# A gated dilated-attention kernel: the transfers of weights, values, queries and keys spread out, and all of feature group 2 by seven products

## The chip, the cores and the metric

The kernel runs on one NeuronCore of one Trainium2 chip. Its time is the device time of an execution in microseconds; before the change three runs gave 748.61, 748.99 and 751.39 us, median 748.99. One further execution was taken with the hardware profiler. The engines are named as the profile names them: PE (TensorE, matrix products), PEld (its weight loads), DVE (VectorE), ACT (ScalarE), POOL (GpSimd) and SP (SyncE, which mostly issues transfers).

## What is computed

x has 2048 positions of 640 features. The reference, cut to what matters:

```python
xn = layernorm(x)
# 32 heads of 20 features, a window of 8 positions, 2 apart, looking back
q, k, v = split(xn @ wqkv)
logits = einsum("bhsd,bhswd->bhsw", q, k[window]) * 20 ** -0.5   # masked before position 0
s = einsum("bhsw,bhswd->bhsd", softmax(logits), v[window]).reshape(1, 2048, 640) @ wo
h = (xn @ w_gate) * (xn @ w_up)          # 1536 features
out = x + s * silu(h @ w_down)
```

## The kernel before

All products run on PE with numbers split into a high and a low part (ACT copies the high part, POOL or DVE subtracts it: L109 and L110 for weights, L1008 and L1012 for attention's output), so a product of two split operands is three matmuls per 128 rows.

**Products by seven.** Several stages treat their matrices as two by two blocks and take seven block products instead of eight (Strassen's scheme). The price is sums and differences of the blocks ahead of the products and additions behind them. `differences` forms the input sums T1 to T4 of four chunks of 512 positions, and stores those of chunks 0 and 1 in main memory (t_scr, and e_scr for T4).

**The stages, in the order of PE's work.** Layernorm statistics and the first feature groups; the q, k, v products in rounds (`qkv`, L428); gate and up for twelve groups of 128 features (`group`, or `gate` and `up`); the output projection in pairs of tiles (`pair_product`, L1033); the down projection by seven products (L896); and the final gating. The input is cut into four chunks of 512 positions.

**Feature groups.** Groups 0 and 1 use plain products. For the groups 3 to 10 `group(f, 2)` takes chunks 2 and 3, then `group(f, 0, 1)` takes chunks 0 and 1, each with seven products: 54 matmuls of 512 columns. Group 2 uses seven products for chunks 2 and 3 and plain products (`gate`, `up`: L119) for chunks 0 and 1: 60 matmuls. `two(f)` says which way a group goes, by the number F_TWO. The weights of a group arrive whole (`load_wf`, 640 KB), `w_add` forms their sums (S and R), `w_split` splits G (gate), U (up), S and R. ACT copies a finished product out (`hold`, L1295), DVE adds and multiplies (`gate_a`, `gate_b` L1298, `up_a`), and `up_b` and `h_b` (L1301, L1304) run on POOL for chunks 2 and 3 and for early groups, on DVE otherwise: `eng = nc.vector if c0 and f >= VEC else nc.gpsimd`. A group's result goes to main memory (h_scr).

**Transfers of T.** `load_t(n)` brings one third of T1 to T3 of chunks 0 and 1 (768 KB) from t_scr, `load_e` half of T4 (512 KB) from e_scr. Both are issued by POOL, in its own order of work.

**Attention.** `attention` is a generator that works through twelve units (a group of heads and one of the two dilation phases, in ORDER) on DVE and POOL: the products q times k (L527), their sums (L534), softmax, then the products with the values (L498) and their accumulation on POOL (L504). One round overlaps the scores of one unit with the values of the unit before. It is not a stage of its own: whoever issues PE work calls `advance(credits)`, and the generator emits steps until its credits are spent. The order of instructions on DVE, POOL and ACT is therefore fixed by where these calls stand. `ahead(n, parts)` issues loads of a unit in SP's queue: part 0 is its queries and keys, part 1 its values, both into two alternating kv buffers. `store_o` writes a unit's result to o_scr.

**Early sums.** `early_sums` forms sums for the T inputs on POOL. EARLY of these steps are issued ahead of `scales(8)` (L278 to L334), whose result PE needs for a product of 32 columns (L340).

**The output projection.** `turn_pair(p)` transposes the two tiles of a pair on DVE (L710) and forms four sums (L982 to L985). `hi_pair` and `lo_pair` split the sums. `split_wo(k)` splits sums of the output weights; `sums_wo` forms them. The pair products' results are added by DVE (L1039 to L1044). `wd_sums` (L797 to L809) prepares the weights of the down projection.

**Dictionaries of places.** `places[second, n]` and `beside[f, second, n]` hold functions that are called behind the n-th product of a group's half (second 0: chunks 2 and 3; second 1: chunks 0 and 1).

Of the kernel before, what the change touches and what calls it, by code (L numbers as in the profile page):

```python
# [19 lines left out]
P = 128  # L20
S, D, F = 2048, 640, 1536
# [23 lines left out]
PACE = 1.0  # L45
VEC = 3
EARLY = 3
GROUP_RATE = 0.184
# [8 lines left out]
def kernel(  # L57
# [316 lines left out]
    ORDER = [0, 1, 2, 3, 4, 6, 5, 7, 8, 11, 9, 10]  # L374
    wide, now = [], [None]
    q_t, kv_t, kv_buf, kv_zero, scr, staged, made = {}, {}, {}, {}, {}, [], set()
# [43 lines left out]
    def qkv(m, r, i, runs=ALL_RUNS, at=None, act=None, bank=("q", 3)):  # L420
# [9 lines left out]
        if m or r:  # L430
            if not staged:
                y = slot([P, 2, 2 * 3 * CMAX], F32)
                staged.extend([y[:, 0], y[:, 1], st([P, 2 * 3 * CMAX], "pk", 1)])
            if c > CMAX and not wide:
                wide.extend([slot([P, 6 * c], F32), st([P, 6 * c], "pk", 1)])
            if i % 2 == 0:
                now[0] = wide if c > CMAX else staged
                now[0].insert(0, now[0].pop())
            n = len(MADE[m])
            y = now[0][0][:, :6 * c].rearrange("p (n a i c) -> p n a i c", n=n, a=3, i=2)  # L440
            nc.scalar.activation(y[:, :, :, i % 2, :].rearrange("p n a c -> p a n c"),
                                 p.rearrange("p (a n c) -> p a n c", a=3, n=n), AF.Copy)
# [18 lines left out]
    def attention():  # L461
# [45 lines left out]
        for n, u in enumerate(ORDER + [None]):  # L507
            if u is not None:
                late_unit = u not in made
                while u not in made:  # L510
                    yield None
                ahead(n, (0, 1))
                for _ in range(5 if late_unit else 0):
# [8 lines left out]
            for j in PAIRS:  # L522
                if u is not None:
                    ahead(n + 1, (0,))
                    k = flat(kv[:, 0, j:j + NE, :])
                    k = bass.AP(k.tensor, k.offset, [k.ap[0], [c, 2], k.ap[1]])
                    nc.vector.tensor_mul(t, q, k)  # L527
                    yield 2 * NE * c * 1.22e-3
# [12 lines left out]
            if u is None:  # L541
                store_o(before)
                ring[:] = three
                return
            ahead(n + 1, (0, 1))
            if before is not None:
# [617 lines left out]
    f0, f1 = KF - 2, KF - 1  # L1164
    F_TWO = 3
    tt, tw, steps = {0: [], 2: []}, {}, []
# [120 lines left out]
    def group(f, c0=0, second=0):  # L1287
# [26 lines left out]
        if not second:  # L1314
            if not two(f - 1):
                w_split(f, "U")
            w_sum.pop(f, None)
            wf_raw.pop(f)
            if f < f1 and f + 1 not in wf_raw:
                load_wf(f + 1)  # L1320
        for n, j in enumerate((0, 5, 2, 1, 4, 3, 6)):
# [18 lines left out]
            if (f, second, n) in beside:  # L1340
                beside[f, second, n]()
            advance(PACE * len(runs) * (GROUP_RATE if two(f) else 0.184))

# [35 lines left out]

    def next_sums(f):  # L1380
        w_split(f, "S", "R")
        w_sum.pop(f)
        if f < f1:
            load_wf(f + 1)

    def first_parts():
# [3 lines left out]
        w_split(2, "S")  # L1390
        yield
        w_split(2, "G")
        yield
# [5 lines left out]
    for m, t in ((m, t) for m in range(1, len(MADE)) for t in range(DIL)):  # L1399
# [3 lines left out]
        for i in range(NE):  # L1403
# [7 lines left out]
            if (m, r, i) == (last - 1, 1, 6):  # L1411
                load_wf(2)
            qkv(m, r, i)
            if i == 1:
                finish_piece()
# [7 lines left out]
        elif (m, r) == (last, 1):  # L1423
            for k in range(2):
# [5 lines left out]
    beside.update({(f0, 0, 5): lambda: advance(1e9), (f0, 1, 0): lambda: begin_last(), (f0, 1, 1): lambda: load_pair(0),  # L1430
                   (f0, 1, 4): lambda: sums_wo(), (f0, 1, 5): lambda: split_wo(0, nc.vector),
                   (f0, 1, 6): lambda: split_wo(1, nc.vector)})

# [15 lines left out]
    def load_late(n):  # L1449
        if n < 2:  # L1450
            load_t(n + 2)
        else:
            load_e(1, n - 2, n - 2)

    for f in range(2, f1):
        places.clear()
        if not two(f):
            places.update({(0, 3): sums("S1", "S2"), (0, 4): sums("S3", "d5", "S4")})
            if two(f + 1):
                places.update({(0, 0): lambda f: load_t(0), (0, 2): lambda f: load_t(1)})  # L1460
            group(f, 2)
            next_sums(f + 1)
            g0 = gate(f, 0)
            g1 = gate(f, 1)
            if two(f + 1):
                tw.pop("G")
            w_split(f + 1, "G")
            up(f, 0, g0)
            up(f, 1, g1)
            if two(f + 1):  # L1470
                tw.pop("U")
# [32 lines left out]
    g3 = gate(f1, 3)  # L1504
    turn_pair(2)
    up(f1, 3, g3)
# [25 lines left out]
    for p in range(SP // 2):  # L1532
# [142 lines left out]
```

## Time and profile before

| | |
|---|---|
| median of three runs | 748.99 us (748.61 to 751.39) |
| profiled execution | 748.28 us |
| its span | 746.5 us |
| PE busy | 735.4 us (99%) |
| DVE busy | 612.2 us (82%) |
| POOL busy | 462.6 us (62%) |
| ACT busy | 302.5 us (41%) |
| granted clock of PE | 1.00 in every stretch asked for |

All times in the text are microseconds from the start of the span. A row of the timeline gives start, duration, engine, line, operation, output<-inputs, the shape and how many instructions were merged; a bracket at its end says how long the engine stood before it, and for whom. A row of the grouped view ends with busy time and mean nanoseconds of one, then the idle time before the group. Names of tiles are those of buffers that are used again and again (s, t, xc, kv, wraw, gh, o), so one name has many uses.

Where the stages lie in this execution: the q, k, v products end at 273.9; chunks 2 and 3 of group 2 run from 273.9 to 286.1, its chunks 0 and 1 from 286.1 to 299.7; groups 3 to 10 follow, with attention beside them until about 489; the pair products run from 525.8 on.

### The profile page before, as it was taken

To read this page: it belongs to the slowest core of one execution; us is meant where nothing else is said; L and a number is where in the kernel's file an instruction comes from. 1 tells how busy PE (TensorE), PEld (TensorE's weight loads), DVE (VectorE), ACT (ScalarE), POOL (GpSimd) and SP (SyncE) were. 2 spreads that over 40 slices of the span, in tenths; PEclk is the share of its full clock that TensorE was granted. 3 is DMA by queue.
4 is the path that set the end of the run, shared out by engine and by line. 5 is a ranking of instruction groups with operands and counts; after the bars stand their busy time and mean duration, and the time that the engine had idled before them with its cause. 6 is when DMAs were issued, how large, how long until landed. Compare 5 with 4: busy or idle time off the path is not lost. (4 is left out here: it accounts for less than half of the span.)

```text
span 746.5 us, 11102 instructions
## 1 busy us (share of the span) xinstructions
PE 735.4 (99%) x4054; PEld 669.0 (90%) x4054; DVE 612.2 (82%) x720; ACT 302.5 (41%) x577; POOL 462.6 (62%) x389
## 2 busy tenths in 40 slices
PE   8999999999999999999999999999999999999997
PEld 6989989988999998778887888887899999999997
DVE  7666998699697887998999999667998777777775
ACT  5658413323332332233223322335556564444442
POOL 6169929787688878888879989877559800000000
PEclk9999999999999999999999999999999999999999
DMA  9465672947446548856165424268567655555534
GB/s 316 170 202 200 236 224 87 299 157 239 127 152 197 190 128 232 274 161 207 55 159 149 115 82 110 72 178 204 167 177 212 228 220 191 191 191 191 191 106 141
DMA packets 103493, 132.98 MB, mean 178 GB/s; under 512 B 22696, under 2 KB 74404, under 8 KB 103438
## 3 DMA queue, kind: packets, MB, share of 16 engines
q1 hardware_dynamic: 84686, 112.77, 48.4%
q10 hardware_dynamic: 17600, 14.26, 5.9%
q0 software_dynamic: 1152, 5.24, 2.2%
q8 instruction: 32, 0.52, 0.3%
q14 instruction: 23, 0.19, 0.1%
HBM read 83.58 MB, written 47.81 MB: 176 GB/s over the span
## 5 line engine op out<-in xcount | busy, mean ns | idle before, releaser
L504 POOL TENSOR_TENSOR o<-o,t 128x960 f32<-128x960 f32 (+1 forms) x69 | 139.6, 2024 | 19.1 <-DVE t L498 17.6
L498 DVE TENSOR_TENSOR t<-e,kv 128x960 f32<-128x960 f32 (+1 forms) x96 | 99.4, 1037 | 24.8 <-POOL o L504 24.7
L527 DVE TENSOR_TENSOR t<-q,kv 128x1920 f32<-128x1920 f32 (+1 forms) x48 | 92.4, 1925 | 4.3 <-DMA kv<-qkv_scr 4.2
L534 DVE TENSOR_REDUCE lg<-t 128x96 f32<-128x1920 f32 (+1 forms) x48 | 92.3, 1922 | 0.2
L428 PE MATMUL q<-s,xc 128*128 128x360 f32 (+1 forms) x450 | 83.1, 334 | 0.6 <-DVE lg L266 0.5
L110 POOL TENSOR_TENSOR s<-wraw,s 128x384 fp32r<-128x384 f32 (+6 forms) x58 | 69.6, 1210 | 19.9 <-ACT s L109 19.9
L428 PEld LDWEIGHTS q<-s,xc 128*128 128x128 f32 x450 | 74.9, 188 | 4.8 <-DVE lg L266 0.8
L1295 ACT ACTIVATE gh<-g 128x512 f32<-128x512 f32 x54 | 32.2, 597 | 115.8 <-PE g L1328 97.8
L428 PE MATMUL u<-s,xc 128*128 128x360 f32 (+1 forms) x360 | 65.8, 334 | 0.0
L428 PEld LDWEIGHTS u<-s,xc 128*128 128x128 f32 x360 | 60.3, 188 | 2.3
L428 PE MATMUL g<-s,xc 128*128 128x360 f32 (+1 forms) x330 | 61.5, 337 | 0.0
L428 PEld LDWEIGHTS g<-s,xc 128*128 128x128 f32 x330 | 55.7, 188 | 2.6
L1328 PE MATMUL u<-xc,s 128*128 128x512 f32 x216 | 55.3, 391 | 0.9 <-ACT gh L1295 0.9
L896 PE MATMUL q<-xc,s 128*128 128x320 f32 x342 | 55.5, 309 | 0.0
L1328 PE MATMUL g<-s,s 128*128 128x512 f32 x216 | 55.0, 390 | 0.0
L896 PEld LDWEIGHTS q<-xc,s 128*128 128x128 f32 x342 | 51.5, 188 | 0.0
L1328 PEld LDWEIGHTS u<-xc,s 128*128 128x128 f32 x216 | 40.3, 188 | 10.5 <-ACT gh L1295 2.0
L1328 PEld LDWEIGHTS g<-s,s 128*128 128x128 f32 x216 | 40.5, 188 | 8.6 <-ACT gh L1295 0.2
L109 ACT ACTIVATE s<-wraw 128x384 fp32r<-128x384 f32 (+6 forms) x59 | 33.5, 587 | 29.5 <-PE g L1328 9.0
L504 POOL TENSOR_TENSOR o<-t 128x960 f32<-128x960 f32 (+1 forms) x12 | 24.4, 2032 | 31.8 <-DVE t L498 25.2
L1328 PE MATMUL g<-xc,s 128*128 128x512 f32 x168 | 41.5, 391 | 1.3 <-ACT gh L1295 1.3
L119 PE MATMUL g<-xc,s 128*128 128x512 f32 (+1 forms) x180 | 40.1, 373 | 0.0
(367 smaller groups left out, 1566.5 us busy)
## 6 DMA issues: line engine op xcount, KB each, us to landing
h_scr<-gh SPq DMA_DIRECT2D x48, 256.0 KB, 2.6
wraw<-in_wgu SPq DMA_DIRECT2D x11, 640.0 KB, 4.4
kv<-qkv_scr SPq DMA_DIRECT2D x14, 480.0 KB, 5.9
qkv_scr<-s ACTq DMA_DIRECT2D x18, 360.0 KB, 4.4
t<-h_scr SPq DMA_DIRECT2D x8, 768.0 KB, 7.1
kv<-qkv_scr SPq DMA_DIRECT2D x14, 367.5 KB, 6.6
s_scr<-gh SPq DMA_DIRECT2D x16, 320.0 KB, 4.2
gh<-s_scr SPq DMA_DIRECT2D x16, 320.0 KB, 3.5
```

The lines of the kernel that those rows point to most:

```text
L109: nc.scalar.activation(hi, raw, AF.Copy)
L110: eng.tensor_sub(lo, raw, hi.bitcast(F32))
L119: nc.tensor.matmul(acc, a, b, start=first and n == 0, stop=last and n == len(runs) - 1)
L428: nc.tensor.matmul(p, xT[(r * NE + i) // TPC][a][:, k, t0:t0 + P], wq[m][b][k], start=n == 0, stop=n == len(runs) - 1, skip_group_check=ac ...
L498: nc.vector.tensor_mul(t.rearrange("p (n d) -> p n d", d=DH), e[:, :, w].unsqueeze(2).to_broadcast([P, NE * nh, DH]), v)
L504: return NE * c * cost, lambda: eng.tensor_add(y, z, t)
L527: nc.vector.tensor_mul(t, q, k)
L534: nc.vector.tensor_reduce(out=lg[:, :, j:j + 2].rearrange("p n a -> p a n"), in_=t.rearrange("p a (n d) -> p a n d", d=DH), op=ALU.add, ax ...
L896: nc.tensor.matmul(p, y[:, i, k], wd_t[name][k][:, l], start=new and r == 0, stop=r == len(runs) - 1, skip_group_check=True)
L1295: nc.scalar.activation(kept[j], b["ACACABA"[j]], AF.Copy)
L1328: nc.tensor.matmul(y, w, x, start=j in (0, 1, 5) and r == 0, stop=r == len(runs) - 1, skip_group_check=True)
```

## The change

1. F_TWO goes from 3 to 2: chunks 0 and 1 of group 2 are taken by `group(2, 0, 1)`, 54 matmuls in place of 60. Group 2's G weights use the single "pk" buffer, which served as a third staging buffer of the q, k, v outputs until then; it leaves that use at the seventh tile from the end of the last round, and G is split at the third from the end.
2. The T transfers come earlier: `load_t(0)` in the last q, k, v round, the second and third load behind the first product of `group(2, 2)`, the fourth behind the second, both `load_e` behind the third. Before, two were issued in `group(2, 2)` and the others in `group(3, 2)`.
3. In attention, the values of a unit are asked for at j = 2 of its own round, and the queries and keys of the next from j = 4 on; before, both were asked for as soon as their buffers allowed, the values at the end of the round before, ahead of that round's store.
4. The weights of a group are asked for behind the first product of the group before it, rather than at its start; those of group 2 in the second last q, k, v round, as before, but the queue's neighbours differ.
5. VEC goes from 3 to 2: `up_b` and `h_b` of group 2's chunks 0 and 1 run on DVE.
6. EARLY goes from 3 to 1.
7. `split_wo(0)` goes one place later, to where `split_wo(1)` stands.
8. `turn_pair(2)` goes from between the last `gate` and `up` to behind `lo_pair(1, 0)` in the first turn of the pair loop.

The program has six matmuls of 512 columns fewer and three DVE additions more.

How the instructions move, at three places. The first is POOL's order around group 2. Line 1182 (1186 after) is a T transfer, the next transfer line an E transfer; L504 (L505) is attention's accumulation, L1272 (L1276) a weight sum, L110 the low part of a split (s: U, S or R; pk: G). Before, from the splits of group 2 on:

```order
L110 TENSOR_TENSOR s_2634<-wraw_2294,s_2634 128x384
L110 TENSOR_TENSOR s_2641<-wraw_2232,s_2641 128x640
L1182 DMA s_2652<-t_scr 128x1536
L389 MEMSET kv_124 1x840
L1182 DMA s_2686<-t_scr 128x1536
L1272 TENSOR_TENSOR wraw_2699<-wraw_2637 128x256
```

and later, in group 3:

```order
L110 TENSOR_TENSOR s_2634<-wraw_2637,s_2634 128x384
L1182 DMA s_2854<-t_scr 128x1536
L389 MEMSET kv_124 1x840
L1182 DMA s_2874<-t_scr 128x1536
L1186 DMA xc_449<-e_scr_109 128x1024
L1186 DMA xc_449<-e_scr_110 128x1024
```

After, in group 2 alone:

```order
L1186 DMA s_2536<-t_scr 128x1536
L505 TENSOR_TENSOR o_2427<-o_2427,t_938 128x640 x2
L110 TENSOR_TENSOR pk_2583<-wraw_2223,pk_2583 128x640
L505 TENSOR_TENSOR o_2427<-o_2427,t_938 128x640 x3
L110 TENSOR_TENSOR s_2633<-wraw_2289,s_2633 128x384
L110 TENSOR_TENSOR s_2633<-wraw_2223,s_2633 128x384
L1186 DMA s_2650<-t_scr 128x1536
L1186 DMA s_2652<-t_scr 128x1536
L1186 DMA s_2665<-t_scr 128x1536
L1190 DMA xc_449<-e_scr_109 128x1024
L1190 DMA xc_449<-e_scr_110 128x1024
```

One T transfer now stands in the last q, k, v round; the three others and both E transfers stand in a row behind group 2's splits.

The second is SP's queue where a unit's store (o_scr) meets the loads for the units that follow (kv: keys or values, q: queries). Before:

```order
L175 DMA wraw_3407<-in_wgu 128x1280
L1284 DMA h_scr<-gh_3324 128x4x128
L1284 DMA h_scr<-gh_3349 128x4x128
L414 DMA kv_124<-qkv_scr_2086 128x960
L416 DMA kv_124<-qkv_scr_2086 112x840
L416 DMA kv_124<-qkv_scr_2086 15x840
L575 DMA o_scr<-o_3163 128x8x80
L575 DMA o_scr<-o_3163 128x8x40
L408 DMA q_3468<-qkv_scr_2463 128x960
L414 DMA kv_1029<-qkv_scr_2463 128x960
```

After:

```order
L175 DMA wraw_3414<-in_wgu 128x1280
L579 DMA o_scr<-o_3154 128x8x80
L579 DMA o_scr<-o_3154 128x8x40
L1288 DMA h_scr<-gh_3408 128x4x128
L1288 DMA h_scr<-gh_3439 128x4x128
L414 DMA kv_124<-qkv_scr_2086 128x960
L416 DMA kv_124<-qkv_scr_2086 112x840
L416 DMA kv_124<-qkv_scr_2086 15x840
L1288 DMA h_scr<-gh_3502 128x4x128
```

The store stands ahead of the value loads, and these two result stores (h_scr) behind it; the next unit's queries come after.

The third is DVE's order at the first pair products. L710 (L714) is a transpose, L982 to L985 (L986 to L989) the four sums of a turn, L797 and L800 (L801, L804) weight sums, L1012 (L1016) a low part, L1039 and L1042 (L1043, L1046) additions of a pair's results. Before:

```order
L985 TENSOR_TENSOR s_4483<-s_4483 128x256
L710 STREAM_TRANSPOSE s_4525<-s_4459 128x640 x2
L982 TENSOR_TENSOR s_4459<-s_4525 128x256
L983 TENSOR_TENSOR s_4459<-s_4459,s_4525 128x256
L984 TENSOR_TENSOR s_4459<-s_4525,s_4459 128x256
L985 TENSOR_TENSOR s_4525<-s_4525 128x256
L797 TENSOR_TENSOR lg_4567<-wraw_4494 128x320
L800 TENSOR_TENSOR lg_4568<-wraw_4494,lg_4567 128x320
L1012 TENSOR_TENSOR xc_4552<-s_4483,xc_4552 128x640
L1039 TENSOR_TENSOR gh_4599<-o_4554,u_4571 128x320
L1042 TENSOR_TENSOR gh_4611<-o_4554,q_2_66 128x320
```

After:

```order
L989 TENSOR_TENSOR s_4478<-s_4478 128x256
L801 TENSOR_TENSOR lg_4555<-wraw_4489 128x320
L804 TENSOR_TENSOR lg_4556<-wraw_4489,lg_4555 128x320
L1016 TENSOR_TENSOR xc_4540<-s_4478,xc_4540 128x640
L714 STREAM_TRANSPOSE s_4569<-s_4454 128x640 x2
L986 TENSOR_TENSOR s_4454<-s_4569 128x256
L987 TENSOR_TENSOR s_4454<-s_4454,s_4569 128x256
L988 TENSOR_TENSOR s_4454<-s_4569,s_4454 128x256
L989 TENSOR_TENSOR s_4569<-s_4569 128x256
L1043 TENSOR_TENSOR gh_4594<-o_4542,u_4559 128x320
L1046 TENSOR_TENSOR gh_4606<-o_4542,q_2_66 128x320
```

The turn of pair 2 (s_4525 before, s_4569 after) now stands between the first low part and the first two additions of results.

The diff, cut to its core:

```diff
-VEC = 3
-EARLY = 3
+VEC = 2
+EARLY = 1
...
-                staged.extend([y[:, 0], y[:, 1], st([P, 2 * 3 * CMAX], "pk", 1)])
+                stage_pk.append(st([P, 2 * 3 * CMAX], "pk", 1))
+                staged.extend([y[:, 0], y[:, 1], stage_pk[-1]])
...
-                ahead(n, (0, 1))
+                ahead(n, (0, 1) if late_unit else (0,))
...
             for j in PAIRS:
                 if u is not None:
-                    ahead(n + 1, (0,))
+                    if j == 2:
+                        ahead(n, (1,))
+                    elif j > 2:
+                        ahead(n + 1, (0,))
...
-            ahead(n + 1, (0, 1))
+            ahead(n + 1, (0,))
             if before is not None:
                 store_o(before)
...
-    F_TWO = 3
+    F_TWO = 2
...
             w_sum.pop(f, None)
             wf_raw.pop(f)
-            if f < f1 and f + 1 not in wf_raw:
-                load_wf(f + 1)
...
                 beside[f, second, n]()
+            if (second, n) == (0, 0) and f < f1 and f + 1 not in wf_raw:
+                load_wf(f + 1)
...
             qkv(m, r, i)
+            if m == last and n == NT - 7:
+                staged[:] = [y for y in staged if y is not stage_pk[-1]]
+            elif m == last and n == NT - 5:
+                load_t(0)
+            elif m == last and n == NT - 3:
+                w_split(2, "G")
...
-                   (f0, 1, 4): lambda: sums_wo(), (f0, 1, 5): lambda: split_wo(0, nc.vector),
-                   (f0, 1, 6): lambda: split_wo(1, nc.vector)})
+                   (f0, 1, 4): lambda: sums_wo(), (f0, 1, 6): lambda: (split_wo(0, nc.vector), split_wo(1, nc.vector))})
...
     def load_late(n):
-        if n < 2:
-            load_t(n + 2)
+        if n == 0:
+            load_t(1)
+            load_t(2)
+        elif n == 1:
+            load_t(3)
         else:
-            load_e(1, n - 2, n - 2)
+            load_e(1, 0, 0)
+            load_e(1, 1, 1)
 
     for f in range(2, f1):
         places.clear()
-        if not two(f):
...
-            group(f, 2)
-            next_sums(f + 1)
-            g0 = gate(f, 0)
-            g1 = gate(f, 1)
...
-            up(f, 0, g0)
-            up(f, 1, g1)
...
-            continue
         places.update(two_places)
         if f == F_TWO:
-            places.update({(0, n): lambda f, n=n: load_late(n) for n in range(4)})
+            for n in range(3):
+                places[0, n] = lambda f, n=n: load_late(n)
         group(f, 2)
         group(f, 0, 1)
...
     g3 = gate(f1, 3)
-    turn_pair(2)
     up(f1, 3, g3)
...
             lo_pair(p + 1, 0)
+            if not p:
+                turn_pair(2)
```

More of the change, by code (lines that the diff above doesn't have):

```diff
@@ L374 @@
     ORDER = [0, 1, 2, 3, 4, 6, 5, 7, 8, 11, 9, 10]
-    wide, now = [], [None]
+    wide, now, stage_pk = [], [None], []
     q_t, kv_t, kv_buf, kv_zero, scr, staged, made = {}, {}, {}, {}, {}, [], set()
@@ L1378, in up @@
         advance(PACE * 2.8)
[L1380 to L1384, printed above, removed]
     def first_parts():
@@ L1390, in first_parts @@
         w_split(2, "S")
-        yield
-        w_split(2, "G")
         yield
@@ L1449, in load_late @@
     def load_late(n):
-        if n < 2:
-            load_t(n + 2)
-        else:
-            load_e(1, n - 2, n - 2)
+        if n == 0:
[3 more added lines that the diff above has]
+            load_t(3)
+        else:
+            load_e(1, 0, 0)
+            load_e(1, 1, 1)
     for f in range(2, f1):
         places.clear()
-        if not two(f):
-            places.update({(0, 3): sums("S1", "S2"), (0, 4): sums("S3", "d5", "S4")})
-            if two(f + 1):
-                places.update({(0, 0): lambda f: load_t(0), (0, 2): lambda f: load_t(1)})
-            group(f, 2)
-            next_sums(f + 1)
-            g0 = gate(f, 0)
-            g1 = gate(f, 1)
-            if two(f + 1):
-                tw.pop("G")
-            w_split(f + 1, "G")
-            up(f, 0, g0)
-            up(f, 1, g1)
-            if two(f + 1):
-                tw.pop("U")
-            continue
         places.update(two_places)
         if f == F_TWO:
-            places.update({(0, n): lambda f, n=n: load_late(n) for n in range(4)})
+            for n in range(3):
+                places[0, n] = lambda f, n=n: load_late(n)
         group(f, 2)
```

## The prediction

> **What bounds the kernel.** I read the head of the page first: the span, the busy time of each engine, and the chain that ended last.
>
> ```profile
> span 746.5 us, 11102 instructions
> ...
> PE 735.4 (99%) x4054; PEld 669.0 (90%) x4054; DVE 612.2 (82%) x720; ACT 302.5 (41%) x577; POOL 462.6 (62%) x389
> ...
> PE 28%; DVE 2%; issue 1%; POOL 1%; DMA 0%; ACT 0%; SPq 0%; DVEq 0%; ACTq 0%
> ```
>
> TensorE is busy for 735.4 of 746.5 us. So a change can gain only in two ways: fewer matmuls, or less of the 11.1 us in which TensorE stands. What it does on DVE, POOL and the queues counts only where TensorE then waits. The second view is therefore who TensorE waited for, as a sum and then in time order.
>
> ```profile
> PE q L224 <- POOL lg masks.py:199: 1.4, 1, 1.4
> PE g L1328 <- ACT gh L1295: 1.3, 2, 0.9
> PE e L340 <- POOL lg L334: 1.0, 1, 1.0
> PE u L1328 <- ACT gh L1295: 0.9, 2, 0.6
> ```
>
> ```profile
> 49.46 0.41 PE L340 MATMUL e<-lg,lg 128*128 128x32 f32 x2 [1.03 <-POOL lg L334]
> ...
> 286.14 3.56 PE L119 MATMUL g<-xc,s 128*128 128x512 f32 x15
> 289.54 3.56 PE L119 MATMUL u<-xc,s 128*128 128x512 f32 x15
> ...
> 323.53 2.35 PE L1328 MATMUL g<-xc,s 128*128 128x512 f32 x9 [0.47 <-ACT gh L1295]
> ...
> 334.34 1.89 PE L1328 MATMUL u<-xc,s 128*128 128x512 f32 x7 [0.30 <-ACT gh L1295]
> ...
> 398.90 1.43 PE L1328 MATMUL g<-xc,s 128*128 128x512 f32 x5 [0.87 <-ACT gh L1295]
> ...
> 508.01 2.34 PE L1328 MATMUL u<-xc,s 128*128 128x512 f32 x9 [0.60 <-ACT gh L1295]
> ...
> 533.96 0.56 PE L1033 MATMUL e<-s,xc 128*128 128x320 f32 x2 [0.78 <-DVE xc L1012]
> 534.75 1.15 PE L1033 MATMUL q<-xc,kv 128*128 128x320 f32 x6 [0.23 <-DVE gh L1042]
> ```
>
> The first wait (1.4 us, at the program's start) isn't touched. The brackets of the timeline, 4.3 us in all, lie where this change works. Every term below is one of these brackets or a new one.
>
> **Six matmuls fewer.** Chunks 0 and 1 of group 2 take 54 matmuls of 512 instead of 60. Fifteen of them last from 286.14 to 289.54, 0.227 us each: 6 x 0.227 = 1.36 us, all on TensorE's path. **-1.36.**
>
> **One early sum instead of three.** L334 lets TensorE go at 49.46.
>
> ```profile
> 43.79 2.55 POOL L593 TENSOR_TENSOR kv<-xc 128x512 f32<-128x512 f32 x2 [17.92 <-DVE xc L370]
> ...
> 47.55 0.21 POOL L278 TENSOR_TENSOR lg<-lg 128x4 f32<-128x4 f32 x1
> ...
> 49.17 0.24 POOL L334 TENSOR_TENSOR lg<-mro,lg 128x32 f32<-128x32 f32 x1
> ```
>
> The scale chain (47.55 to 49.41) stands behind three sums on POOL (43.79 to 47.55). Two of them, 2.5 us, go behind it, so it ends near 46.9; TensorE would arrive at 49.46 - 1.03 = 48.43. The wait goes whole. The sums put back are not late next: the same POOL work stands between this chain and the next. **-1.03.**
>
> **The T loads.** They move from group 3 to group 2: T1 to T3 of chunks 0 and 1 are now read in group 2's second half, which starts at 286.14. POOL issues the second, third and fourth load and both E loads in one go, behind the R and U splits.
>
> ```profile
> 261.20 1.56 POOL L110 TENSOR_TENSOR s<-wraw,s 128x640 fp32r<-128x640 f32 x1
> ...
> 277.45 2.55 POOL L110 TENSOR_TENSOR s<-wraw,s 128x384 fp32r<-128x384 f32 x2
> ```
>
> ```profile
> L1182 POOL DMA_DIRECT2D s<-t_scr x4: 527/564/758, 279.9 to 307.9; - x4
> ...
> DMA to landing us min/median/max: 8.8/10.6/11.7
> ```
>
> The 2.55 us are a split of 384 columns and one of 640; the second alone is 1.56, so 384 cost 0.99. Both are 384 wide afterwards and end at 277.45 + 1.98 = 279.4. Issues follow at 0.56 us (the median of the L1182 row): 279.4, 280.0, 280.5. TensorE reads the second load in its third product, at 286.14 + 15 x 0.227 = 289.54, the third two matmuls later, at 290.0, the fourth after 15 more, at 292.9. With the shortest landing all are there: no wait. With the median the third comes at 290.6 (0.6 us), with the longest at 291.7 (1.7 us). The loads go out in a row, so I take a value between the median and the longest. **+1.0, ends 0 and +1.7.**
>
> [...]
>
> **What the old T transition cost.** ACT held its copies back at 323.53 and 334.34, where group 3 reads the T tiles for the first time with its stores behind their loads: 0.77 us together. The same crowd now stands in group 2. I take half as moved. **-0.4, ends -0.77 and +0.4.**
>
> **The order in SP's queue.** The store of an attention round now goes ahead of the next value load.
>
> ```profile
> 392.59 2.26 POOL L504 TENSOR_TENSOR o<-t 128x960 f32<-128x960 f32 x1 [5.39 <-DMA o_scr<-o]
> ```
>
> POOL stood 5.39 us for that store; its weight sums and gate additions queue behind, then ACT's copy, then TensorE at 398.90. With the store first there is nothing of this left. **-0.87, ends -0.87 and 0.**
>
> The keys of the next unit are asked for later, from j = 4, and the values of a unit at j = 2 of its own round. Here the bound is DVE's work until they are read.
>
> ```profile
> L527 DVE TENSOR_TENSOR t<-q,kv 128x1920 f32<-128x1920 f32 (+1 forms) x48 | 92.4, 1925 | 4.3 <-DMA kv<-qkv_scr 4.2
> L534 DVE TENSOR_REDUCE lg<-t 128x96 f32<-128x1920 f32 (+1 forms) x48 | 92.3, 1922 | 0.2
> ...
> kv<-qkv_scr SPq DMA_DIRECT2D x14, 480.0 KB, 5.9
> ```
>
> A step of two offsets is at least 1.93 (L527) + 1.92 (L534) = 3.85 us of DVE. Two steps remain for the keys (7.7 us), three for the values (11.5 us), against 5.9 us to landing: **0.** With the cover gone DVE would stand for kv, as in the 4.2 us at L527 above.
>
> **split_wo(0) one place later.** The wait at 508.01 comes through POOL's L1304.
>
> ```profile
> 504.03 0.81 DVE L110 TENSOR_TENSOR s<-t,s 128x640 fp32r<-128x640 f32 x1
> 504.77 0.68 DVE L1298 TENSOR_TENSOR gh<-gh,u 128x512 f32<-128x512 f32 x1
> ...
> 505.58 1.75 POOL L1304 TENSOR_TENSOR gh<-gh,gh 128x512 f32<-128x512 f32 x1 [2.15 <-issue]
> ```
>
> L1298 comes at 504.03 instead, 0.74 us earlier, which would cover all of the 0.60. But the sums ahead of it wait for weights loaded after the attention's end, which the later loads can push back. **-0.4, ends -0.6 and +0.6.**
>
> **Group 2 on DVE and POOL.** Seven products bring three DVE additions more and take two off POOL (VEC).
>
> ```profile
> 274.00:300.00 26.00, 26.00 (x117) 21.52 (x116) 20.33 (x25) 8.53 (x15) 22.80 (x21) 1.00 0.82 232
> 300.00:350.00 50.00, 49.14 (x213) 39.36 (x212) 47.52 (x52) 16.12 (x27) 40.50 (x37) 1.00 0.73 217
> ```
>
> DVE (third column of busy time) has 5.7 us free in 274 to 300. An addition of this width takes 0.68 (L1298 above), five of them 3.4 us: hidden. **0.** After 300 only 2.5 of 50 us are free, so a delay of DVE beyond that would reach TensorE.
>
> **turn_pair(2) moved behind lo_pair(1, 0).** This is the term I trust least. The wait at 533.96 is for L1012, which stands behind turn_pair(2) on DVE; moved, L1012 runs some 2.7 us earlier and the two waits of 533.96 and 534.75 (1.0 us, and 1.34 with the late starts around them) go. But the turn now stands ahead of the additions L1039 and L1042 of the first pair, in a stretch where POOL works, as the start times of the next two fences show.
>
> ```profile
> 523.41 1.67 DVE L983 TENSOR_TENSOR t<-t,s 128x256 f32<-128x256 f32 x1
> ...
> 527.73 1.56 DVE L710 STREAM_TRANSPOSE s<-s 128x640 f32<-128x640 f32 x2
> ...
> 529.78 0.42 DVE L983 TENSOR_TENSOR s<-s,s 128x256 f32<-128x256 f32 x1
> ...
> 532.41 1.50 DVE L1012 TENSOR_TENSOR xc<-s,xc 128x640 fp32r<-128x640 f32 x1
> 533.82 0.47 DVE L1039 TENSOR_TENSOR gh<-o,u 128x320 f32<-128x320 f32 x1
> ```
>
> ```profile
> 523.06 1.74 POOL L110 TENSOR_TENSOR xc<-o,xc 128x640 fp32r<-128x640 f32 x1
> ...
> 532.10 1.12 POOL L110 TENSOR_TENSOR kv<-wraw,kv 128x320 fp32r<-128x320 f32 x1
> 533.18 1.44 POOL L110 TENSOR_TENSOR xc<-lg,xc 128x320 fp32r<-128x320 f32 x1
> ```
>
> The same addition takes 0.42 us while POOL stands and 1.67 where a POOL split runs: it ends just after the split. DVE is free at 527.73; two weight sums and L1012 (1.50 us there beside a split, some 0.8 estimated without) go first, until about 530.5, then the transposes, 1.56 us, until 532.1. Three of the four additions meet the splits up to 533.18 + 1.44 = 534.6, the fourth ends near 535.4, and L1039 and L1042 (0.47 each: L1039 in the DVE rows above ran at that price beside a split) near 536.3. TensorE, no longer stopped at 533.96, wants that result at 533.6 (L1042 ended near 534.7 and TensorE still waited 0.23, so without the first stop of 0.78 and its late start of 0.16 it would ask at 534.75 - 0.23 - 0.94): 2.7 us, less the 1.34 that go. **+1.3.** If the additions took 0.42 us each, L1042's would end at 534.6: 1.0 - 1.34 = **-0.3** is the one end; one split more in the way is the other, **+2.0.**
>
> **Sum:** -1.36 - 1.03 + 1.0 - 0.4 - 0.87 - 0.4 + 1.3 = -1.76 us. The profiled execution took 748.28 us (746.5 of span and 1.8 around it), 0.7 below the median of the runs, 748.99, and is the lowest seen: 748.28 - 1.76 = **746.5**. About 0.5% of this kernel, 3.74 us, is what a measurement can tell from no change: bounds 745.25 and 752.73.
>
> **Rivals.** (1) T hidden and the turn free: all waits go. -1.36 - 1.03 - 0.77 - 0.87 - 0.6 - 0.3 = -4.9: **743.3**, faster. For it: the shortest landing is early enough, and splits that come 2.5 us earlier or later would be out of the turn's way. Against: the median of the four landings, and splits back to back from 532.1 to 534.6 just where the turn goes. (2) The opposite: five loads on one queue share the transfer engines. The share of these in 274 to 300 is already 0.82 at 232 GB/s (232 KB per us; last columns above). Three T loads, 2.36 MB, with half of that need 20 us: the third lands near 297, TensorE stands 7 us, and 746.5 - 1.0 + 7 = **752.5**; past 297.3 the kernel is slower by over 0.5%. Against: no T load took over 11.7 us. (3) The key and value loads come late and the attention slips by a microsecond or more in each of five units; DVE's 2.5 us per 50 absorb some, the end of the attention shifts by about 2, and the wait at 508 grows by that: **748.5**, no change.
>
> **Chances.** Forecast (744.5 to 748.0) 0.42; rival 1 0.33; rival 3 0.12; rival 2, with other new waits of that size, 0.13. The lowest part of the forecast's own range lies under 745.25, and a part of rival 2 stays under 752.73: faster 0.37, within 0.5% 0.51, slower 0.12. The range runs from rival 1 with its waits a little better still, 742.0, to 750.5, which leaves out rival 2.
>
> **What would show it.** 4048 matmuls on the page; no wait at L334's reader near 48; the brackets on ACT's copies gone near 322, 333 and 397. A wait of TensorE in group 2's third product near 289, its releaser the T load, is the T term. At 533 to 537 a wait for the gate additions with DVE additions of over 1 us ahead of it is the turn; additions of 0.42 there are rival 1. A DVE wait for kv is rival 3. I am wrong if TensorE waits much at a place not named here, above all for DVE between 300 and 490.

## The result and the profile after

The change made the kernel slower: 754.58 us (median of 6 runs, 752.57 to 755.79) against 750.31 us for the kernel before (6 runs). The ratio is 1.0068, 95% interval 1.0052 to 1.0085. Forecast were 746.5 us and a range up to 750.5. The profiled execution took 752.57 us.

The head of the page of the changed kernel, and its row of span and clock:

```profile
span 750.8 us, 11098 instructions
...
PE 736.0 (98%) x4048; PEld 670.0 (89%) x4048; DVE 618.3 (82%) x723; ACT 303.0 (40%) x579; POOL 462.8 (62%) x389
...
PE 30%; DVE 2%; DMA 1%; issue 0%; ACT 0%; DVEq 0%; ACTq 0%
```

```profile
core 0: 750.8 us, clock 0.994
```

Six matmuls are gone, and yet TensorE is busy 0.6 us longer: its granted clock, 1.000 over the span before, is 0.994 here. TensorE's waits in the changed kernel, as a sum and then in time order:

```profile
PE g L1330 <- ACT gh L1299: 2.5, 1, 2.5
PE u L1330 <- ACT gh L1299: 2.2, 2, 1.2
PE q L1037 <- DVE gh L1046: 1.9, 1, 1.9
PE u L119 <- ACT pk L442: 1.8, 1, 1.8
PE q L224 <- POOL lg masks.py:199: 1.4, 1, 1.4
```

```profile
89.91 5.30 PE L119 MATMUL u<-xc,s 128*128 128x512 f32 x15 [1.81 <-ACT pk L442]
...
408.23 2.11 PE L1330 MATMUL u<-xc,s 128*128 128x512 f32 x8 [1.16 <-ACT gh L1299]
...
458.51 1.67 PE L1330 MATMUL u<-xc,s 128*128 128x512 f32 x6 [1.02 <-ACT gh L1299]
...
512.36 1.85 PE L1330 MATMUL g<-xc,s 128*128 128x512 f32 x6 [2.52 <-ACT gh L1299]
...
539.26 1.14 PE L1037 MATMUL q<-xc,kv 128*128 128x320 f32 x6 [1.88 <-DVE gh L1046]
```

Every wait that the prediction set out to remove is gone: those at 49, 323, 334, 398, 508 and the two at 534 to 535. Five others stand in their place. Two of these carry a second cost, which the 15 matmuls at 89.91 show: they last 5.30 us, where 15 in a row took 3.56 before. The view by stretches (the third figure from the end is the granted clock) shows why:

```profile
91.00:94.00 3.00, 3.00 (x9) 2.37 (x8) 2.96 (x2) 1.83 (x4) 2.36 (x1) 0.53 1.05 395
94.00:97.00 3.00, 3.00 (x15) 2.47 (x14) 2.74 (x3) 0.00 (x0) 2.73 (x4) 1.00 0.91 264
...
514.00:517.00 3.00, 3.00 (x8) 2.32 (x7) 3.00 (x6) 2.10 (x3) 1.71 (x2) 0.50 0.59 176
```

Behind the waits of 1.81 and 2.52 us the granted clock was 0.50, from 90.41 to 93.82 and from 513.66 to 517.07. Seven or eight matmuls of 512 columns took 0.427 us each there, from start to start, instead of 0.227: 1.4 us and 1.6 us more.

The account from the two profiles, each wait counted from the time at which the next matmul would have started: 1.36 us of matmuls and 5.4 us of the prediction's waits (their brackets sum to 4.3) went; 9.2 us of new waits (brackets 8.4) and 3.0 us of slow matmuls came. That makes +5.4 us; the span grew by 4.3. Two stops of 0.2 us at 301 and 307 went too; some 0.7 us is left over in pieces too small to name.

### The profile page after: what moved, and what is told of

It reads as the page before. It is cut to its first block, busy times and chain, and to the rows that moved or that the text cites. A ratio compares the mean times of both kernels' runs of the same rounds, so it can differ in the third digit from the quotient of the medians.

```text
span 750.8 us, 11098 instructions
## 1 busy us (share of the span) xinstructions
PE 736.0 (98%) x4048; PEld 670.0 (89%) x4048; DVE 618.3 (82%) x723; ACT 303.0 (40%) x579; POOL 462.8 (62%) x389
## 5 line engine op out<-in xcount | busy, mean ns | idle before, releaser
L505 POOL TENSOR_TENSOR o<-o,t 128x960 f32<-128x960 f32 (+1 forms) x69 | 139.7, 2024 | 12.5 <-DVE t L499 11.7
L1299 ACT ACTIVATE gh<-g 128x512 f32<-128x512 f32 x57 | 34.1, 598 | 117.9 <-PE g L1330 109.2
L110 POOL TENSOR_TENSOR s<-wraw,s 128x384 fp32r<-128x384 f32 (+6 forms) x57 | 68.7, 1218 | 20.5 <-ACT s L109 20.3
L1330 PE MATMUL u<-xc,s 128*128 128x512 f32 x228 | 58.4, 391 | 2.2 <-ACT gh L1299 2.2
L1330 PE MATMUL g<-s,s 128*128 128x512 f32 x228 | 58.0, 390 | 0.0
L1330 PEld LDWEIGHTS u<-xc,s 128*128 128x128 f32 x228 | 42.6, 188 | 12.4 <-ACT gh L1299 3.5
L1330 PEld LDWEIGHTS g<-s,s 128*128 128x128 f32 x228 | 42.7, 188 | 9.0 <-ACT gh L1299 0.2
L505 POOL TENSOR_TENSOR o<-t 128x960 f32<-128x960 f32 (+1 forms) x12 | 24.4, 2034 | 30.0 <-DVE t L499 28.2
L1330 PE MATMUL q<-xc,pk 128*128 128x512 f32 x171 | 41.9, 389 | 0.0
```

The lines of the kernel that those rows point to most:

```text
L110: eng.tensor_sub(lo, raw, hi.bitcast(F32))
L505: return NE * c * cost, lambda: eng.tensor_add(y, z, t)
L1299: nc.scalar.activation(kept[j], b["ACACABA"[j]], AF.Copy)
L1330: nc.tensor.matmul(y, w, x, start=j in (0, 1, 5) and r == 0, stop=r == len(runs) - 1, skip_group_check=True)
```

## Experiments

All ratios are to the kernel before, run beside the kernel on the same chip, with 95% intervals. A difference between two ratios carries both intervals: between the change and an experiment that is about 0.2%, or 1.6 us.

| Run | What it is | Ratio | Interval |
|---|---|---|---|
| the change | | 1.0068 | 1.0052 to 1.0085 |
| e1_early3 | change, EARLY back at 3 | 1.0041 | 1.0028 to 1.0055 |
| e2_early1_then5 | change, one sum first, five right behind the chain | 1.0041 | 1.0029 to 1.0054 |
| e3_split_back | change, split_wo(0) back | 1.0001 | 0.9990 to 1.0012 |
| e4_turn_back | change, turn_pair(2) back | 1.0027 | 1.0014 to 1.0040 |
| e5_before_early1 | before, EARLY = 1 alone | 1.0018 | 1.0006 to 1.0030 |
| e7_before_split_late | before, split_wo(0) moved alone | 1.0016 | 1.0005 to 1.0026 |
| e11_before_turn_late | before, turn_pair(2) moved alone | 1.0018 | 1.0006 to 1.0029 |
| e8_e_load_later | change, one E transfer later | 1.0033 | 1.0020 to 1.0046 |
| e6_three_back | change, the three small moves back | 0.9966 | 0.9954 to 0.9978 |
| e12_loads_back | as e6, attention's loads back too | 1.0037 | 1.0023 to 1.0050 |
| e9_phase | as e6, attention one step earlier | 0.9955 | 0.9943 to 0.9967 |
| e10_early_phase | as e9, and e2's early sums | 0.9949 | 0.9936 to 0.9962 |

### EARLY

```diff
-EARLY = 1
+EARLY = 3
```

> The changed kernel with EARLY back at 3. Theory: with EARLY = 1 POOL forms two sums later, so the stores of T come later; ACT's store of q, k, v waits for one of them, ACT's next copy stands behind that store, and TensorE stands 1.8 us at 89.9 and runs at half clock behind it. So that stop and the slow matmuls go (about -3.4 us) and the wait of 1.0 us for L334 near 49 comes back (+1.2): 2.2 us faster than the changed kernel, 1.004 of the kernel before. Rival: the stop at 89.9 comes from another part (the loads of queries and keys, the weights' load); it stays, and the time is 1.2 us longer than the changed kernel's, 1.008.

Measured 1.0041, that is 0.27% or 2.0 us below the change; 2.2 were expected. The stop at 89.9 and its slow matmuls are gone, the wait of 1.0 for L334 near 49 is back. (Its profile has slow matmuls behind two later stops, at 511, where five took 2.50 us, and at 538, where six of 320 columns took 1.82; the change's has them behind one, at 512, and at 539 six of 320 columns took 1.14.) The path of the stop is in ACT's rows. In the changed kernel:

```profile
88.41 0.52 ACTq L446 DMA_DIRECT2D qkv_scr<-s  x1
89.03 0.47 ACT L442 ACTIVATE pk<-g 128x360 f32<-128x360 f32 x1 [8.62 <-DMA t_scr<-t]
```

and in the kernel before:

```profile
85.38 0.52 ACTq L445 DMA_DIRECT2D qkv_scr<-s  x1
86.00 0.47 ACT L441 ACTIVATE pk<-g 128x360 f32<-128x360 f32 x1 [3.82 <-DMA t_scr<-t]
```

ACT's store of q, k, v has nothing to do with the T store on SP. In the trace ACT's queue waits for semaphore 102, which the T store uses too (the transfers of SP and ACT use eight in this program, 101 to 106, 108 and 109), and its store goes out, at 88.41, when the T store has landed, at 88.33. ACT's copy of a finished product queues behind it, and TensorE's next product wants that buffer. The same wait, 3.82 us, was there before and cost nothing, because TensorE came 1.8 us later and the T store landed at 85.30. Of these 3.0 us the T store's later issue (84.20 instead of 83.14) is 1.1; the rest is its landing, which took 3.8 to 4.1 us in the change, e3, e4 and e5, all with EARLY = 1, and 2.1 to 2.2 in the kernel before, e1 and e2. Why it lands more slowly is not shown. The part alone, on the kernel before:

```diff
-EARLY = 3
+EARLY = 1
```

> The kernel before with EARLY at 1 and nothing else. Theory: the wait near 49 goes (-1.2), the stop at 89.9 appears by this part alone, 1.6 to 2.0 us, with half clock behind it if it is long enough (1.4 more): 0.4 to 2.2 us slower than the kernel before, 1.0005 to 1.003. Rival: the stop needs the later loads of keys and queries too; here the gain stands alone, 1.2 us faster, 0.998.

Measured 1.0018 (1.4 us, interval 0.4 to 2.2): slower by this part alone. The stop at 89.67 is 1.55 us in its profile, without slow matmuls (six took 1.65 us), more than the 1.03 that went. So it needs neither group 2 nor attention's loads, and the rival is out. How much of the 1.4 us is this stop is not shown: the same profile has a stop of 1.90 us with slow matmuls at 325 (five took 2.35 us), where e11, with the old program up to there, has one of 1.94. In the second form, the chain goes first but no sum is put off for long:

```diff
-    for _ in range(3):
+    for _ in range(5):
         next(early)
```

> The changed kernel, one sum ahead of the scale chain as in it, but five right behind the chain in place of three, so that as many sums stand ahead of the next products as before the change. Theory: what costs is that two sums were put off for long, not that the chain goes first. Both waits (49 and 89.9) are gone: 3.4 us faster than the changed kernel, 1.002 of the kernel before. Rival: TensorE arrives at 89.9 some 1.8 us earlier than before the change, and that alone makes the store late; a stop of 0.5 to 1.8 us stays there, 1.004 to 1.007.

Measured 1.0041. The stop at 89.9 is gone, as the theory has it, but a new wait of 0.6 us stands before the next chain's reader near 55.6: the sums now stand ahead of that chain. 2.0 us were gained, not 3.4.

### split_wo(0)

```diff
-(f0, 1, 6): lambda: (split_wo(0, nc.vector), split_wo(1, nc.vector))
+(f0, 1, 5): lambda: split_wo(0, nc.vector),
+(f0, 1, 6): lambda: split_wo(1, nc.vector)
```

> The changed kernel with split_wo(0) back at its place ahead of gate_b. Theory: with gate_b first, POOL's h_b runs beside the two splits on DVE, which take 1.7 us each in place of 0.8; up_a and its store come 0.7 us later, land 2.6 us later, ACT's copy waits for the buffer, TensorE stands 2.5 us at 512 and runs at half clock behind it. With the old order the splits take 0.8 us, the stop at 512 goes (about -4.2) and one of 0.6 to 0.8 us at 508 comes back: 3.5 us faster than the changed kernel, 1.002 of the kernel before. Rival: the store lands late because of the loads beside it; the stop at 512 stays at 2 us or more, 1.006 to 1.008.

Measured 1.0001: 0.67%, or 5.0 us below the change, more than the 3.5 expected. Not all of it is the edit's doing: the stop at 89.6 was 1.49 us here, without slow matmuls (six took 1.66 us), which saves 1.7 us in all, and an edit at 502 can't have caused that; at 534 a stop of 2.16 us had slow matmuls behind it, which cost 1.2. By these ratios this single place of two small operations was still the largest part of the loss. What it did in the changed kernel, on DVE and ACT:

```profile
502.85 0.67 DVE L1302 TENSOR_TENSOR gh<-gh,u 128x512 f32<-128x512 f32 x1
503.44 3.42 DVE L110 TENSOR_TENSOR s<-t,s 128x640 fp32r<-128x640 f32 x2
506.79 0.68 DVE L1315 TENSOR_TENSOR gh<-gh,g 128x512 f32<-128x512 f32 x1
...
511.71 0.60 ACT L1299 ACTIVATE gh<-g 128x512 f32<-128x512 f32 x1 [4.57 <-DMA h_scr<-gh]
```

gate_b (L1302) comes first and frees POOL, as intended. POOL then works beside the two splits, which take 1.7 us each instead of 0.81 in the kernel before; up_a (L1315) starts 0.51 us behind the first of the six products that TensorE begins at 506.28, instead of 0.21 before. Its store goes out at 507.49 and takes until 511.61 to land, 4.12 us instead of 2.19 before, and ACT's next copy needs that store's buffer. TensorE waits for this copy. Alone, on the kernel before:

```diff
-(f0, 1, 5): lambda: split_wo(0, nc.vector),
-(f0, 1, 6): lambda: split_wo(1, nc.vector)
+(f0, 1, 6): lambda: (split_wo(0, nc.vector), split_wo(1, nc.vector))
```

> The kernel before with split_wo(0) moved to the place of split_wo(1) and nothing else. Theory: the wait of 0.6 at 508 goes, and one of 2.5 us with half clock behind it (1.6) appears near 512, by this part alone: 3.4 us slower, 1.0045. Rival: the stop appears only where TensorE comes early through the other parts; 0.7 us faster to 0.7 slower, 0.999 to 1.001.

Measured 1.0016 (1.2 us; 0.4 to 2.0). The new stop is there as expected, 2.22 us with slow matmuls behind it (seven took 2.44 us), but the whole time rose by less than 3.4 us. So the stop belongs to this part alone, and its price depends on what the rest does: here the waits at the pair products, 1.6 us before, are gone as well. Which link makes the store late, the DVE order or the transfers beside it, was tried with the E transfer of POOL:

```diff
-... lo_pair(0, 1), load_e(3, 1, 3)), (f1, 0, 5): sum_w5,
-                   (f1, 0, 3): lambda: load_e(3, 0, 2)})
+... lo_pair(0, 1), load_e(3, 0, 2), load_e(3, 1, 3)),
+                   (f1, 0, 5): sum_w5})
```

> The changed kernel with POOL's first E transfer of chunk 3 (512 KB) issued behind the sixth product's work, beside the second one, so that it can't go ahead of the two stores that ACT waits for at 512. Theory A: the stores (issued at 507.5 to 508.0) land 4 us after their issue because POOL, free earlier, issued that transfer 1.4 us ahead of them; now they land in 2.2 to 2.9 us, the stop at 512 falls below 1.2 us and the half clock goes: 2.9 to 3.7 us faster than the changed kernel, 1.002 to 1.003. Theory B: the stores are late because up_a waits behind the two slow splits on DVE; the stop stays at 2 us or more with its half clock, 1.006 to 1.007.

Measured 1.0033, 0.35% or 2.6 us below the change, between the two theories. The profile has two more differences, which about cancel: no slow matmuls behind the stop of 1.44 us at 90.1 (eight took 2.12 us), and slow ones behind the stop at 536. TensorE's waits there:

```profile
PE u L1330 <- ACT gh L1299: 2.4, 2, 1.4
PE q L1037 <- DVE gh L1046: 2.2, 1, 2.2
PE g L1330 <- ACT gh L1299: 1.8, 1, 1.8
```

The stop fell from 2.52 to 1.76 us, and no slow matmuls stand behind it (five took 1.42 us). The store still took 3.35 us to land (506.76 to 510.11). In the five profiles in which POOL issues the E transfer 1.4 us ahead of it (the change, e1, e2, e4, e7) it took 3.80 to 5.28 us; in the three in which the transfer goes out behind it (before, e3, e6) 2.19. So the E transfer issued ahead is one cause; that up_a, 0.3 us later, is another is argued, not shown, and why the store takes 3.35 us with no E transfer in the way stays open.

### turn_pair(2)

```diff
     g3 = gate(f1, 3)
+    turn_pair(2)
     up(f1, 3, g3)
...
-            if not p:
-                turn_pair(2)
```

> The changed kernel with turn_pair(2) back between the last gate and up. Theory: the turn beside POOL's splits costs 0.91 to 0.98 us per addition in place of 0.42 and holds L1046 up; undone, the stop of 1.9 us at 539 goes and the two of 0.78 and 0.23 (1.3 with the late starts) come back: 0.7 us faster than the changed kernel, 1.006 of the kernel before. Rival: the waits at the first pair depend on what POOL splits there, not on the turn; no difference or up to 0.5 us slower.

Measured 1.0027, 3.1 us below the change rather than 0.7. Its profile has no wait at all at the pair products, and no slow matmuls behind the stop of 1.45 us at 89.5 (six took 1.67 us), which this edit can't have caused. The stop at 511 was 3.69 us here, time in which DVE could get ahead; e7, the other kernel with that stop and the old turn, has no wait at the pair products either, but that this is the reason is argued, not shown. So the run says little on the turn by itself. The part alone, on the kernel before:

```diff
     g3 = gate(f1, 3)
-    turn_pair(2)
     up(f1, 3, g3)
...
             lo_pair(p + 1, 0)
+            if not p:
+                turn_pair(2)
```

> The kernel before with turn_pair(2) moved and nothing else. Theory: the waits of 0.94, 0.40 and 0.24 us at 534 to 537 go and one of 2.0 to 2.3 us for L1042 appears near 535, with the turn's additions at 0.9 to 1.0 us beside POOL's splits: 0.5 to 0.75 us slower, 1.001. The prediction had +1.3 us for this term. Rival: the turn is free there; 0.3 us faster or more, 0.9995 or less, with additions of 0.42 us.

Measured 1.0018 (1.4 us; 0.4 to 2.2): slower, where the rival had it faster. The additions beside POOL's splits, in the changed kernel, DVE first and then POOL:

```profile
535.14 0.91 DVE L986 TENSOR_TENSOR s<-s 128x256 f32<-128x256 f32 x1
536.09 0.98 DVE L987 TENSOR_TENSOR s<-s,s 128x256 f32<-128x256 f32 x1
537.11 0.97 DVE L988 TENSOR_TENSOR s<-s,s 128x256 f32<-128x256 f32 x1
538.00 0.41 DVE L989 TENSOR_TENSOR s<-s 128x256 f32<-128x256 f32 x1
```

```profile
534.89 0.88 POOL L110 TENSOR_TENSOR xc<-wraw,xc 128x320 fp32r<-128x320 f32 x1 [2.87 <-ACT xc L109]
535.73 1.06 POOL L110 TENSOR_TENSOR kv<-wraw,kv 128x320 fp32r<-128x320 f32 x1
536.75 1.05 POOL L110 TENSOR_TENSOR xc<-lg,xc 128x320 fp32r<-128x320 f32 x1
```

Three additions meet three splits, each ending just after its split, and the fourth takes 0.41, as the prediction laid it out. TensorE's wait for the additions behind them was 2.16 us in e11 and 1.88 in the change. Counted from the time the next matmul would have started, e11 lost 2.6 us there and the kernel before 1.6: 1.0 us more. The rest of the measured 1.4 us may lie elsewhere: that profile also has a stop of 1.94 us and slow matmuls at 324 (seven took 2.46 us), where its program is that of the kernel before.

### What the rest of the change is worth

EARLY, split_wo(0) and turn_pair(2) as before, the rest as changed:

> The changed kernel with EARLY at 3, split_wo(0) and turn_pair(2) at their old places: what is left is group 2 by seven products with its T transfers, the order of attention's loads, the weights' load and VEC. Theory: these three parts cost 2.3, 3.7 and 0.7 us of the changed kernel's time; the rest gains the six matmuls and the waits of 300 to 400, less two stops of 1.2 to 1.5 us near 406 and 456: 6.7 us faster than the changed kernel, 2 us or so faster than the kernel before, 0.997 to 0.998. Rival: the rest costs too (T transfers, loads); 1.000 or more.

Measured 0.9966 (0.9954 to 0.9978), 746.39 us against 748.81: 2.4 to 2.5 us faster than the kernel before. The three small moves together thus cost 1.0068 - 0.9966 = 1.02%, 7.6 us. Alone on the kernel before they cost 1.4, 1.2 and 1.4 us, 4.0 in sum; that they cost more together is not split up further. Its waits:

```profile
PE u L1330 <- ACT gh L1299: 2.6, 3, 1.4
PE q L224 <- POOL lg masks.py:199: 1.4, 1, 1.4
PE e L340 <- POOL lg L334: 1.0, 1, 1.0
PE e L1037 <- DVE xc L1016: 0.8, 1, 0.8
```

No wait for a T transfer, none between 50 and 406. The weights' load and VEC were not tried alone. Attention's loads were then put back into their old order as well:

```diff
-                ahead(n, (0, 1) if late_unit else (0,))
+                ahead(n, (0, 1))
...
-                    if j == 2:
-                        ahead(n, (1,))
-                    elif j > 2:
-                        ahead(n + 1, (0,))
+                    ahead(n + 1, (0,))
...
-            ahead(n + 1, (0,))
+            ahead(n + 1, (0, 1))
```

> The kernel with three parts back, and attention's loads asked for as in the kernel before (values ahead of the store, keys from the first step). Theory: the store of a round lands 5 us later behind the value loads, POOL stands for it and TensorE stands 0.9 to 1.0 us near 397: 0.9 us slower than the kernel with three parts back, 0.998. Rival: these loads made no difference beside group 2's seven products; the same time, 0.9966.

Measured 1.0037: 0.71% or 5.3 us slower than with the new order, not 0.9. Both the stop behind the late store and a new one are there:

```profile
292.34 1.20 PE L1327 MATMUL g<-s,s 128*128 128x512 f32 x4 [2.44 <-DMA s<-t_scr]
...
401.68 0.50 PE L1327 MATMUL g<-xc,s 128*128 128x512 f32 x1 [2.37 <-ACT gh L1296]
```

each with slow matmuls behind it (the granted clock of this execution was 0.995, that of e6 1.000). The first is the T wait of the prediction. The view of the T transfers' line in e12, and then in e6:

```profile
L1183 POOL DMA_DIRECT2D s<-t_scr x4: 535/557/758, 265.0 to 280.3; - x4
...
DMA to landing us min/median/max: 5.7/10.9/13.9
```

```profile
L1186 POOL DMA_DIRECT2D s<-t_scr x4: 537/560/758, 264.9 to 280.2; - x4
...
DMA to landing us min/median/max: 5.5/8.4/10.3
```

POOL issues them at the same times; with the value loads out of their way they land in 10.3 us at most, with them in it in 13.9. With the attention loads in their old order the rest of the change loses more than it gains, 1.0037 against 0.9966.

### The two stops at 406 and 456

```diff
         group(f, 0, 1)
+        if f == F_TWO:
+            advance(1.26)
```

> The kernel with three parts back (EARLY 3, split_wo(0), turn_pair(2)), and 1.26 credits more given to attention once, behind group 2: what the plain products of group 2 gave it beyond the seven. Theory: with the fewer credits attention runs one step later, so one of its accumulations (2.3 us on POOL) stands between up_b and h_b in the groups whose stops are at 406 and 456; one step earlier it stands ahead of up_b, and the two stops (1.5 and 1.0 us) go: 2.5 us faster than the kernel with three parts back, 0.993 of the kernel before. Rival: POOL is full in these stretches, the accumulation only moves the wait to another copy of ACT; 0.995 to 0.997.

Measured 0.9955; the interval (0.9943 to 0.9967) overlaps that of e6. The stops at 406 and 456 went, so their cause, an accumulation of attention (L505) standing between up_b (L1305) and h_b (L1308) on POOL, is shown. POOL in e6, and then in e9:

```profile
401.93 2.27 POOL L505 TENSOR_TENSOR o<-o,t 128x960 f32<-128x960 f32 x1
404.15 1.29 POOL L1308 TENSOR_TENSOR gh<-gh,gh 128x512 f32<-128x512 f32 x1
```

```profile
399.72 2.27 POOL L505 TENSOR_TENSOR o<-o,t 128x960 f32<-128x960 f32 x1
401.94 1.30 POOL L1305 TENSOR_TENSOR gh<-gh,gh 128x512 f32<-128x512 f32 x1
...
404.17 1.29 POOL L1308 TENSOR_TENSOR gh<-gh,gh 128x512 f32<-128x512 f32 x1
```

But one of 0.91 us came at 307, one of 0.25 at 332, and the one of 0.41 at 505 grew to 0.77:

```profile
307.10 2.11 PE L1330 MATMUL u<-xc,s 128*128 128x512 f32 x8 [0.91 <-ACT gh L1299]
```

In time the rival's reading comes nearer: most of the wait moved. With e2's early sums on top:

> The kernel of e9_phase with one sum ahead of the scale chain and five right behind it. Theory: the wait of 1.2 us near 49 gives way to one of 0.7 near 55.6, as in e2_early1_then5, and nothing is late at 89.9: 0.5 us faster than e9_phase, 0.992 to 0.993. Rival: TensorE, half a microsecond earlier, meets later waits for as much; the same time as e9_phase.

Measured 0.9949 (0.9936 to 0.9962), 745.30 us against 749.36 beside it: the fastest kernel here, faster than the kernel before and the change. In its profile the wait near 49 gave way to one of 0.6 near 56. Its lead over e9 is within both intervals.

## Why the prediction was wrong, by its steps

- **Six matmuls, -1.36.** Right: 4048 matmuls, and no plain product in group 2.
- **One early sum, -1.03.** The wait went, but "The sums put back are not late next" was wrong. The step looked at the next chain only. The two sums delay the T stores, and one of these, landing 3.0 us later, holds ACT's store. The part costs +1.4 us alone and 2.0 in the change.
- **T transfers, +1.0.** No wait; landings of 5.6 to 10.6 us were at the good end of the bound. The prediction took the old landings although the change also moves the loads that go out beside them; e12 shows the price with the old order (13.9 us at most to landing, 10.3 in e6), a stop of 2.44 us and slow matmuls behind it (three took 1.11 us instead of 0.84), which is rival 2 in kind at a third of its size.
- **The old T transition, -0.4.** It went whole. The profiled execution also understated it: two kernels whose program is unchanged up to there (e7, e11) had 1.76 and 1.94 us at that place, where the profile of before had 0.47.
- **The order in SP's queue, -0.87.** Right in sign and place; 5.3 us by e12 when T comes early as well.
- **Group 2 on DVE and POOL, 0.** No wait there. But the fewer credits of group 2, which the prediction did not cost at all, let attention run one step later, and two stops of 1.16 and 1.02 us stand at 408 and 458 for it.
- **split_wo(0), -0.4.** This step failed most. It counted the 0.74 us by which gate_b comes earlier, and not what POOL does with them: it works beside both splits (a split of its own, then h_b), so that up_a, which stands behind both in either order, comes 0.3 us later, and it issues its E transfer ahead of up_a's store instead of behind it. The store lands in 4.12 us instead of 2.19. The wait at 508 went, and one of 2.52 us with a granted clock of 0.50 behind it came at 512: 5.0 us by the ratios in the change, 1.2 us alone.
- **turn_pair(2), +1.3.** Right in mechanism: 1.88 us of wait where 2.7 were laid out, against brackets of 1.0 (1.6 with all late starts).
- **No step had the clock.** All waits were priced at their own length. Two of the five stops cost 1.4 to 1.6 us more each, the granted clock being 0.50 behind them. Behind stops of like length it was 0.50 in one profile and 1.00 in another, as the last section shows.

The prediction's own sign of being wrong, a wait of TensorE at a place that it did not name, came at 89.9, 408, 458 and 512. Rival 1 was right in its first half, T hidden; with split_wo(0) and turn_pair(2) undone and attention in phase, e10 comes to 745.3. The rival that went slower named one mechanism; three others, each in a part that looked like a small adjustment, made the loss.

## What to carry to other kernels

When a wait is removed, ask what the work put behind is late for two steps on, across queues: here a store of ACT's waited for the semaphore of a T store with which it shares no data, and went out at 88.41, when that had landed, at 88.33. A move that lets an engine run earlier also moves what it does next, work beside another engine's (splits of 0.81 us that became 1.7) or a transfer ahead of another, so look at what that now meets. Price a stop of TensorE with the slow matmuls that may follow it (1.4 and 1.6 us here, behind stops of 1.81 and 2.52), and test small adjustments one by one, since here the large parts gained 2.5 us and three small ones lost 7.6.

## What the hardware showed that was not expected

Behind some short stops TensorE's granted clock was 0.50, and the length of a stop alone does not tell behind which. In the changed kernel it was 0.50 from 90.41 to 93.82, behind the stop of 1.81 us, and from 513.66 to 517.07, behind that of 2.52; behind the stops of 1.16 us at 408 and of 1.88 us at 539 it stayed at 1.00. The stop of 1.88 us at the pair products, which left the clock alone in the change, was followed by a clock of 0.50 in e1. One of 2.16 us left it alone in e11, and in e3 one of 2.16 us was followed by slow matmuls that cost 1.2 us. (The ends of matmuls are modelled in the profile, so these lengths are approximate.) What else decides is not shown.

```profile
324.00:326.00 2.00, 1.92 (x7) 1.56 (x8) 2.00 (x3) 1.18 (x3) 1.16 (x1) 0.79 0.02 4
326.00:329.00 3.00, 3.00 (x10) 2.36 (x9) 2.72 (x3) 0.53 (x1) 3.00 (x3) 0.57 0.00 0
...
540.00:543.00 3.00, 2.91 (x20) 2.65 (x19) 1.58 (x3) 2.90 (x7) 0.00 (x0) 1.00 0.72 220
```

```profile
537.60 1.82 PE L1037 MATMUL q<-xc,kv 128*128 128x320 f32 x6 [1.88 <-DVE gh L1046]
```

```profile
537.90:541.10 3.20, 3.20 (x14) 3.20 (x14) 2.45 (x5) 0.88 (x2) 0.00 (x0) 0.50 0.22 85
```

The first fence shows stretches of e11, behind its stops of 1.94 us (324; clock 0.57 in 326 to 329) and 2.16 us (538; 1.00); the other two show the stop of 1.88 us in e1 and the stretch behind it (0.50).

In both places where DVE's work was put beside POOL's it became slower: an addition of 0.42 us took 0.91 to 0.98 beside a split, and a split of 0.81 us on DVE took 1.7 beside POOL's split and h_b.
